# Second feed-forward's up part as seven block products, and 384-token groups throughout

## The chip, the core and the metric

The kernel runs on one core of a Trainium2 chip. The metric is the device time of one execution in microseconds (us). The core has TensorE (matmuls, PE; its weight loads are shown apart as PEld), VectorE (DVE), ScalarE (ACT), GpSimd (POOL) and SyncE (SP), which issues the transfers. Each engine runs its own queue in order; an instruction that needs another engine's result waits at the head of its queue, and everything behind it waits too.

## What is computed

Three parts follow each other on 1536 tokens (two sequences of 768) of width 320.

```python
x = mlstm(q, k, v, i_gate, f_gate, o_gate)          # gated linear attention, 8 heads of 40
x = x.transpose(0, 2, 1, 3).reshape(1536, 320)
# first feed-forward, d_ff = 1536
xn = x / sqrt(mean(x * x) + 1e-6) * rms_g
g, val = xn @ w_gate, xn @ w_val
x = (g * sigmoid(g) * val) @ w_out
# second feed-forward, d_ff = 2048
h = x @ w_in                                         # "up": 320 -> 2048
out = maximum(0.01 * h, h) @ w_out2                  # "down": 2048 -> 320
```

All is float32. The kernel keeps float32 accuracy with TensorE's faster `float32r` type by splitting each operand into a rounded part (`h`, "high") and the remainder (`l`, "low") and adding three products: high x high, high x low, low x high.

## The kernel before

**Tokens and hidden units.** The 1536 tokens are 12 tiles of 128. The first feed-forward treats hidden blocks 0 to 7 in four groups of three tiles (384 tokens, `GA`), and hidden blocks 8 to 11 in three groups of four tiles (512 tokens, `GB`). The second feed-forward uses `GB` too: 3 groups of 512 tokens, 16 hidden blocks of 128.

**The up part of the second feed-forward** (`h_up`, line 568 through `up`): for each group and hidden block one chain of eight matmuls of 512 columns into one PSUM bank. Input width 320 is two blocks of 128, which take three matmuls each (rows 0 to 255 of the weight), and a rest of 64, whose high and low parts share one 128-row tile (`w[:, 4]`, two matmuls). ACT then applies the leaky maximum (`h_relu`, line 684), ACT rounds the result (`sh`, line 607) and DVE subtracts to get the remainder (`sl`, line 613). The first feed-forward's up part (tiles `g` and `v`) has the same eight-matmul chain in the same function.

**The down part** (`out_down`, lines 697 to 699): per hidden block and 128-token tile three matmuls of 320 columns. Eight hidden blocks are added up in PSUM (`oa`), then kept in SBUF: the first half by an ACT copy, the second half by a DVE addition (`out_keep`, lines 707 and 709). That is 12 copies and 12 additions in all. Then `out_store` sends each tile out.

**PSUM** has eight banks, used as four pairs by tags `gv`, `o`, `acc`, `s`.

**Weights** arrive as 64-bit floats and are turned into float32 by three steps (`to_f32`: a DVE shift, an ACT rescale, a DVE merge), then split by an ACT cast and a DVE subtraction. `weight_a` makes the up weights (`wA`), `weight_b` the down weights (`wB`), `weight_r` the rest tiles.

**The order of the work** is the text `ORDER`: a list of tokens such as `H.0.3` (up of group 0, block 3), `R`, `S`, `L` (leaky maximum, rounding, remainder), `O` (down), `OK` (keep), `dO` (store). `play` calls them one by one, and each engine executes its share in just that order.

Of the kernel before, what the change touches and what calls it, by code (L numbers as in the profile page):

```python
# [7 lines left out]
F32 = mybir.dt.float32  # L8
# [33 lines left out]
GB = ((0, 4), (4, 8), (8, 12))  # L42
# [35 lines left out]
T.1.5 av.10.0 av.10.1 E.1.5 inn.10 abs.10 rec.10 th.10 y1.10 yr.10 U.1.5.1 M.1.5 arg.11.0 S.1.5 S.1.7 U.2.2.0 L.1.5
T.2.2 L.1.7 U.2.1.0 T.2.1 E.2.1 sq.10 p.11.1 E.2.2 de.11 xn.9 D.1.1.0 K.1.1.0 U.2.1.1 M.2.1 U.2.2.1 S.2.1 M.2.2
U.2.0.0 L.2.1 T.2.0 E.2.0 D.1.1.2 K.1.1.2 wA.9 U.2.0.1 M.2.0 D.1.1.1 y2.10.0 S.2.2 y2.10.1 K.0.1.1 K.1.1.1 b.9 th.11  # L80
eq.11 S.2.0 L.2.0 U.2.3.0 T.2.3 L.2.2 U.2.3.1 xc.9 tp.9 xh.9 p.11.0 av.11.0 av.11.1 wR.5 E.2.3 M.2.3 S.2.3 y2.10.2
inn.11 L.2.3 D.2.0.1 abs.11 rec.11 y1.11 yr.11 sq.11 K.2.0.1 D.2.0.0 xn.10 D.2.0.2 y2.11.0 xc.10 xl.9 y2.11.1 y2.11.2
xn.11 xc.11 tp.10 tp.11 close U.2.4.0 a.10 a.10 wA.8 a.8 b.9 a.8 wR.4 xh.10 U.2.5.0 xl.10 wA.12 T.2.4 E.2.4 U.2.4.1
M.2.4 xh.11 xl.11 S.2.4 L.2.4 b.9 a.8 a.8 T.2.5 E.2.5 U.2.7.0 r.4 U.2.5.1 U.3.2.1 a.12 r.4 r.4 U.3.2.0 T.2.7 M.2.5
a.12 K.2.0.0 E.2.7 r.4 U.2.7.1 M.2.7 U.2.6.0 a.12 S.2.5 L.2.5 a.9 a.9 S.2.7 U.2.6.1 T.2.6 E.2.6 M.2.6 U.3.0.1 S.2.6
a.12 wA.14 K.2.0.2 U.3.0.0 L.2.6 L.2.7 D.2.1.2 a.9 T.3.2 E.3.2 wA.17 M.3.2 U.3.3.0 D.2.1.0 T.3.0 a.14 a.14 a.9 K.2.1.2
a.14 wB.8 a.14 E.3.0 M.3.0 r.5 wA.11 S.3.0 L.3.0 wR.6 a.17 T.3.3 D.2.1.1 E.3.3 U.3.3.1 r.5 S.3.2 M.3.3 a.17 S.3.3
# [36 lines left out]
def body(ctx: ExitStack, tc, ig, fg, qk, nat, wgv, wgr, wo1, wi2, wi2r, wo2, rg, cst, cst2, out):  # L124
# [407 lines left out]
    def weight_b(key):
# [9 lines left out]
        else:  # L542
            w = slot("wB", [128, 2 * DM], key - NF, f"wB_{key}")
# [282 lines left out]
```

## Time and profile before

| | |
|---|---|
| median of three runs | 461.98 us (460.37 to 462.34) |
| the profiled execution | 458.02 us, of which 456.2 us from its first to its last instruction |
| mean granted TensorE clock | 0.977 |
| PE busy | 441.6 us (97%), 3566 instructions |
| DVE busy | 270.4 us (59%), 593 instructions |
| ACT busy | 232.3 us (51%), 549 instructions |
| POOL busy | 53.1 us (12%), 86 instructions |

Busy time of PE is not the measure of a matmul's cost here: the trace gives each 512-column matmul a duration of 395 ns, but they overlap, and what counts is the distance from one start to the next. The second feed-forward's up matmuls run from 267 us to about 440 us, mixed with the down matmuls.

### The profile page before, as it was taken

To read this page: it belongs to the slowest core of one execution; us is meant where nothing else is said; L and a number is where in the kernel's file an instruction comes from. 1 tells how busy PE (TensorE), PEld (TensorE's weight loads), DVE (VectorE), ACT (ScalarE), POOL (GpSimd) and SP (SyncE) were. 2 spreads that over 40 slices of the span, in tenths; PEclk is the share of its full clock that TensorE was granted. 3 is DMA by queue.
4 is the path that set the end of the run, shared out by engine and by line. 5 is a ranking of instruction groups with operands and counts; after the bars stand their busy time and mean duration, and the time that the engine had idled before them with its cause. 6 is when DMAs were issued, how large, how long until landed. Compare 5 with 4: busy or idle time off the path is not lost.

```text
span 456.2 us, 8986 instructions
## 1 busy us (share of the span) xinstructions
PE 441.6 (97%) x3566; PEld 393.6 (86%) x3568; DVE 270.4 (59%) x593; ACT 232.3 (51%) x549; POOL 53.1 (12%) x86
## 2 busy tenths in 40 slices
PE   9977979999999999999999999999999999999996
PEld 5764879999999999998887888988988888989896
DVE  5698998688776678785767785434603222221331
ACT  4686857666752365474435445544634444153150
POOL 4434552431110100000000000000000000000000
PEclk8579999999999999999999999999999999999999
DMA  7899894855810014331142110010101000010201
GB/s 284 298 303 269 274 317 121 252 191 140 215 70 1 2 55 171 109 99 57 35 146 98 31 57 30 29 30 0 59 0 31 29 2 0 1 43 1 72 1 58
DMA packets 21034, 45.43 MB, mean 100 GB/s; under 512 B 2128, under 2 KB 9168, under 8 KB 20992
## 3 DMA queue, kind: packets, MB, share of 16 engines
q1 hardware_dynamic: 20992, 44.85, 31.3%
q8 instruction: 28, 0.46, 0.4%
q14 instruction: 14, 0.11, 0.1%
HBM read 42.79 MB, written 2.06 MB: 98 GB/s over the span
## 4 chain that ended last, share of the span: by engine, by line
PE 91%; DVE 4%; ACT 2%; issue 1%; ACTq 0%; DVEq 0%
PE h L568 20%; PE g L568 15%; PE v L568 14%; PE xa L631 10%; PE oa L699 6%; PE oa L697 6%; PE oa L698 6%; PE xw L649 5%; PE s L290 2%; PE o L350 1%; PE A L216 1%; PE busy L181 1%; PE o L360 1%; DVE w L337 1%; ACT w L306 1%
## 5 line engine op out<-in xcount | busy, mean ns | idle before, releaser
L568 PE MATMUL h<-X,wA 128*128 128x512 f32 x384 | 93.2, 395 | 0.0
L568 PEld LDWEIGHTS h<-X,wA 128*128 128x128 f32 x384 | 71.4, 188 | 15.7
L613 DVE TENSOR_TENSOR sl<-u,sh 128x512 fp32r<-128x512 f32 x48 | 32.8, 691 | 87.0 <-ACT sh L607 87.0
L568 PE MATMUL v<-X,wA 128*128 128x384 f32 (+1 forms) x352 | 73.7, 355 | 1.5 <-ACT X L458 0.7
L568 PE MATMUL g<-X,wA 128*128 128x384 f32 (+1 forms) x352 | 74.1, 355 | 0.0
L568 PEld LDWEIGHTS v<-X,wA 128*128 128x128 f32 x352 | 62.5, 188 | 6.6 <-DVE th L601 1.0
L568 PEld LDWEIGHTS g<-X,wA 128*128 128x128 f32 x352 | 62.2, 188 | 5.2 <-DVE th L597 0.6
L684 ACT ACTIVATE u<-h 128x512 f32<-128x512 f32 x48 | 28.6, 598 | 67.5 <-PE h L568 55.3
L698 PE MATMUL oa<-wB,sh 128*128 128x320 f32 x192 | 59.3, 309 | 0.0
L699 PE MATMUL oa<-wB,sl 128*128 128x320 f32 x192 | 59.3, 309 | 0.0
L697 PE MATMUL oa<-wB,sh 128*128 128x320 f32 x192 | 59.3, 309 | 0.0
L631 PE MATMUL xa<-sh,wB 128*128 128x384 f32 x160 | 45.6, 337 | 0.0
L607 ACT CAST sh<-th 128x384 fp32r<-128x384 f32 (+1 forms) x44 | 23.5, 542 | 36.4 <-DVE th L601 30.3
L698 PEld LDWEIGHTS oa<-wB,sh 128*128 128x128 f32 x192 | 36.0, 188 | 0.9
L697 PEld LDWEIGHTS oa<-wB,sh 128*128 128x128 f32 x192 | 36.0, 188 | 0.9
L607 ACT CAST sh<-u 128x512 fp32r<-128x512 f32 x48 | 29.6, 620 | 13.6 <-PE oa L698 12.6
L699 PEld LDWEIGHTS oa<-wB,sl 128*128 128x128 f32 x192 | 36.0, 188 | 0.0
L590 ACT ACTIVATE th<-g 128x384 f32<-128x384 f32 (+1 forms) x44 | 22.9, 520 | 25.3 <-PE g L568 20.9
L601 DVE SCALAR_TENSOR_TENSOR th<-th,v 128x384 f32<-128x384 f32 (+1 forms) x44 | 25.8, 589 | 12.6 <-PE v L568 11.4
L631 PE MATMUL xa<-sl,wB 128*128 128x384 f32 x96 | 32.3, 336 | 0.0
L597 DVE SCALAR_TENSOR_TENSOR th<-th,g 128x384 f32<-128x384 f32 (+1 forms) x44 | 25.8, 586 | 9.7 <-ACT th L590 9.7
L631 PEld LDWEIGHTS xa<-sh,wB 128*128 128x128 f32 x160 | 29.3, 188 | 0.4
(111 smaller groups left out, 605.5 us busy)
## 6 DMA issues: line engine op xcount, KB each, us to landing
raw_B<-wo SPq DMA_DIRECT2D x28, 320.0 KB, 3.0
qkt<-qk SPq DMA_DIRECT2D x12, 512.0 KB, 6.7
raw_A<-wgv SPq DMA_DIRECT2D x12, 512.0 KB, 5.6
nat<-nat SPq DMA_DIRECT2D x12, 484.0 KB, 6.9
Ab<-A_d SPq DMA_DIRECT2D x10, 512.0 KB, 6.4
raw_A<-wi SPq DMA_DIRECT2D x8, 512.0 KB, 3.7
eb<-e_d SPq DMA_DIRECT2D x20, 128.0 KB, 8.0
out<-x SPq DMA_DIRECT2D x12, 160.0 KB, 1.9
```

The costliest lines, as they stand in the source:

```text
L568: PE.matmul(dst, a, x, start=(i == 0), stop=(i == len(seq) - 1))
L590: A.activation(th, u[0], AF.Tanh, scale=0.5)
L597: V.scalar_tensor_tensor(out=u["t"], in0=u["t"], scalar=1.0, in1=u[0], op0=ALU.add, op1=ALU.mult)
L601: V.scalar_tensor_tensor(out=u["t"], in0=u["t"], scalar=0.5, in1=u[1], op0=ALU.mult, op1=ALU.mult)
L607: A.copy(u["h"], u["t"])
L613: V.tensor_tensor(u["l"], u["t"], u["h"].bitcast(F32), op=ALU.subtract)
L631: PE.matmul(xa, w, x, start=(k == 0), stop=(k == len(seq) - 1))
L649: PE.matmul(xas["w", g, i], a, x, start=(f == NE and k == 0), stop=(f == NF - 1 and k == len(seq) - 1),)
L684: A.activation(t, u[0], AF.Prelu, alpha=0.01)
L697: PE.matmul(dst, sh[:, ts], wb[:, 0:DM], start=first, stop=False)
L698: PE.matmul(dst, sh[:, ts], wb[:, DM:], start=False, stop=False)
L699: PE.matmul(dst, sl[:, ts], wb[:, 0:DM], start=False, stop=last)
```

## The change

The up part of the second feed-forward now treats two groups of 384 tokens (a pair) and two blocks of 128 hidden units together. With weights `a11, a12` (to the first hidden block) and `a21, a22` (to the second), the second digit being the input block, and inputs `b11, b21` (first group) and `b12, b22` (second group), the 2 x 2 x 2 block product of the 256 main inputs takes seven products of blocks instead of eight (Strassen's scheme in Winograd's form). A product still is three matmuls. It needs sums of weight blocks (`s1` to `s4`, made by GpSimd), sums of input blocks (`t1` to `t4`, made by DVE) and running sums of products: bank `u[0]` accumulates one product after another, and is copied out by ACT three times in between (`c11`, `c21`, `c22`), and DVE adds the other banks to these copies (`h_sum`). The 64 rest inputs keep their two matmuls per hidden block and group.

Around that: `GB` is now `GA` (384 tokens everywhere, four groups); the outer loop of the second feed-forward is over 8 pairs of hidden blocks for all tokens, so a down chain adds up two hidden blocks in PSUM and is then kept, 8 times per tile (12 ACT copies and 84 DVE additions); the up weights of the second feed-forward are made one pair of hidden blocks after the other and reuse 8 + 4 slots; more buffers (`TB`, `SBL` = 8); and `ORDER` is another list from its 572nd token on (`M.0.7` before). Of it one line is shown.

```diff
-GB = ((0, 4), (4, 8), (8, 12))
+GB = GA
+PAIRS = ((0, 1), (2, 3))
+NK = DFF2 // 256
+SBL = 8
+TB = 8
...
-X.2.0 X.2.1 H.2.4 R.1.5 S.1.17 L.1.17 O.1.5 b.22 b.23 R.2.4 S.2.16 H.2.1 R.2.1 S.2.13 L.2.13 O.1.6 H.2.2 O.1.7
+R.1.0.3 H.0.1.1 OK.0.0.3 R.1.0.1 S2.1.0.1 X.1.1 L2.1.0.1 S2.1.0.3 R.1.0.2 O.0.0.1 H.0.1.0 HS.0.1.0 L2.1.0.3 X.1.6
...
+    def weight_s(key):
+        x = yield from to_f32(raws["A", key], 512, f"A{key}")
+        ...
+        G.tensor_tensor(q[0], a21, a22, op=ALU.add)
+        G.tensor_tensor(q[1], q[0], a11, op=ALU.subtract)
+        G.tensor_tensor(q[2], a11, a21, op=ALU.subtract)
+        G.tensor_tensor(q[3], a12, q[1], op=ALU.subtract)
+        A.copy(a[:, 0:128], a11)
+        A.copy(a[:, 128:384], x[:, 1])
+        V.tensor_tensor(a[:, 384:512], a11, a[:, 0:128].bitcast(F32), op=ALU.subtract)
+        V.tensor_tensor(a[:, 512:768], x[:, 1], a[:, 128:384].bitcast(F32), op=ALU.subtract)
+        ...
+        A.copy(a[:, 768:896], q[0])
+        A.copy(b[:, 0:384], sc[:, 128:512])
+        V.tensor_tensor(a[:, 896:1024], q[0], a[:, 768:896].bitcast(F32), op=ALU.subtract)
+        V.tensor_tensor(b[:, 384:768], sc[:, 128:512], b[:, 0:384].bitcast(F32), op=ALU.subtract)
...
+    def product(dst, k, p, a, b, first, last):
+        (ah, al), (bh, bl) = LEFT[NF + k][a], RIGHT[p][b]
+        for j, (x, y) in enumerate(((ah, bh), (ah, bl), (al, bh))):
+            PE.matmul(dst, x, y, start=first and j == 0, stop=last and j == 2, skip_group_check=not first)
+    def rest(dst, k, p, m, e, again):
+        PE.matmul(dst, w, X[:, 2, cs], start=False, stop=False, skip_group_check=again)
+        PE.matmul(dst, w, X[:, 5, cs], start=False, stop=True, skip_group_check=again)
...
-    def h_up(g, f):
-        cs, w = span(GB[g])
-        us[g, NF + f] = {0: psum(f"h{g}_{f}", "gv" if f % 2 else "o")[:, 0:w]}
-        up(us[g, NF + f][0], WA[NF + f // 2], f % 2, cs)
+    def h_up(k, p, i):
+        if i == 0:
+            product(h_bank(k, p, 0), k, p, "a11", "b11", True, True)
+        elif i == 1:
+            product(h_bank(k, p, 1), k, p, "s3", "t3", True, True)
+        elif i == 2:
+            product(h_bank(k, p, 2), k, p, "a12", "b21", True, False)
+            rest(u[2], k, p, 0, 0, False)
+        elif i == 3:
+            product(u[0], k, p, "s2", "t2", False, True)
+        elif i == 4:
+            product(h_bank(k, p, 3), k, p, "a22", "t4", True, False)
+            rest(u[3], k, p, 1, 0, False)
+        elif i == 5:
+            product(u[0], k, p, "s1", "t1", False, True)
+        elif i == 6:
+            rest(u[1], k, p, 1, 1, True)
+        else:
+            product(u[0], k, p, "s4", "b22", False, False)
+            rest(u[0], k, p, 0, 1, True)
+    def h_sum(k, p, i):
+        if i == 0: A.copy(u["c11"], u[0])
+        elif i == 1: V.tensor_tensor(u["c11"], u[2], u["c11"], op=ALU.add)
+        elif i == 2: A.copy(u["c21"], u[0])
+        elif i == 3: V.tensor_tensor(u["c21"], u[1], u["c21"], op=ALU.add)
+        elif i == 4: V.tensor_tensor(u["c21"], u[3], u["c21"], op=ALU.add)
+        elif i == 5: A.copy(u["c22"], u[0])
+        else: V.tensor_tensor(u["c22"], u[1], u["c22"], op=ALU.add)
...
+    def out_down(k, p, i):
+        for m in range(2):
+            PE.matmul(oa, v["h"][:, ts], wb[:, 0:DM], start=m == 0, stop=False)
+            PE.matmul(oa, v["h"][:, ts], wb[:, DM:], start=False, stop=False)
+            PE.matmul(oa, v["l"][:, ts], wb[:, 0:DM], start=False, stop=m == 1)
+    def out_keep(k, p, i):
+        if k == 0: A.copy(dst, oas[k, p, i])
+        else: V.tensor_tensor(dst, oas[k, p, i], dst, op=ALU.add)
```

TensorE before, about halfway through the second feed-forward: `h` is an up bank, `oa` a down bank, `wA` and `wB` the weights; the brackets name the engine whose result a row waits for.

```order
L568 MATMUL h_0_4280<-X,wA_2733 128x512 [waits Activation_49]
L568 MATMUL h_0_4280<-X,wA_2733 128x512 x7
L568 MATMUL h_5_4297<-X,wA_2832 128x512 x8
L568 MATMUL h_13_4308<-X,wA_3460 128x512 [waits Activation_49]
L568 MATMUL h_13_4308<-X,wA_3460 128x512 x7
L697 MATMUL oa_0_0_4323<-wB_3300,sh_12_4291 128x320 [waits Activation_49]
L698 MATMUL oa_0_0_4323<-wB_3300,sh_12_4291 128x320
L699 MATMUL oa_0_0_4323<-wB_3300,sl_12_4293 128x320 [waits DVE_49]
L697 MATMUL oa_0_1_4327<-wB_3300,sh_12_4291 128x320
L698 MATMUL oa_0_1_4327<-wB_3300,sh_12_4291 128x320
L699 MATMUL oa_0_1_4327<-wB_3300,sl_12_4293 128x320
```

Three whole chains of eight stand behind each other, each into a bank of its own, and a chain waits only for its bank to come free, before its first matmul.

TensorE now, the start of hidden pair 5 (the behind `h` stand the token pair, the bank and a serial number; `wS` and `T` hold the sums of weights and of inputs):

```order
L780 MATMUL h_0_2_5046<-X,wA_4704 128x384 x3
L785 MATMUL h_0_2_5046<-X,wA_4704 128x384
L786 MATMUL h_0_2_5046<-X,wA_4704 128x384
L780 MATMUL h_0_1_5055<-T_4_3680,wS_4986 128x384 [waits Activation_49]
L780 MATMUL h_0_1_5055<-T_5_3711,wS_4986 128x384
L780 MATMUL h_0_1_5055<-T_4_3680,wS_4986 128x384 [waits DVE_49]
L780 MATMUL h_0_0_5030<-T_4_3680,wS_4986 128x384 x3
L780 MATMUL h_0_3_5063<-T_5_3711,wA_4704 128x384 x3
L785 MATMUL h_0_3_5063<-X,wA_4704 128x384
L786 MATMUL h_0_3_5063<-X,wA_4704 128x384
L780 MATMUL h_0_0_5030<-X,wA_4704 128x384 [waits Activation_49]
L780 MATMUL h_0_0_5030<-X,wA_4704 128x384 x2
```

A chain is now cut into pieces: bank 0 takes three matmuls, then five into bank 3, and then three into bank 0 again, which wait for ACT's copy of what it held.

ACT now, the same place (`c` the copies and running sums, `u` and `c` also the leaky maximum's results, `xh` the rounded ones, `raw` and `w` the weights):

```order
L842 ACTIVATE c_4_1_4968<-c_4_1_4968 128x384 [waits DVE_49]
L615 CAST wB_5024<-w_B_4918 128x320
L820 COPY c_5_0_5034<-h_0_0_5030 128x384 [waits PE_49]
L842 ACTIVATE u_1_1_5044<-h_1_0_4876 128x384 [waits PE_49]
L847 CAST xh_1_1_5052<-u_1_1_5044 128x384 [waits Activation_49]
L825 COPY c_5_0_5069<-h_0_0_5030 128x384 [waits PE_49]
L531 ACTIVATE raw_R_4812<-raw_R_4812 128x256 [waits DMAHW0_49]
L832 COPY c_5_0_5081<-h_0_0_5030 128x384 [waits PE_49]
L597 CAST wA_5097<-w_R_5073 64x256 [waits DVE_49]
L597 CAST wA_5098<-w_R_5073 64x256
L842 ACTIVATE c_5_0_5034<-c_5_0_5034 128x384
```

The three copies of line 820, 825 and 832, on which TensorE's next product depends, stand in one queue with the leaky maximum of the unit before and with weight conversions.

ACT before, in its second feed-forward:

```order
L684 ACTIVATE u_6_4030<-h_6_4015 128x512 [waits DVE_49,PE_49]
L607 CAST sh_18_4032<-u_6_4030 128x512 [waits Activation_49]
L684 ACTIVATE u_0_4045<-h_0_4036 128x512 [waits DVE_49,PE_49]
L607 CAST sh_12_4047<-u_0_4045 128x512 [waits Activation_49]
L493 ACTIVATE raw_B_3960<-raw_B_3960 128x320 [waits DMAHW3_49]
L684 ACTIVATE u_3_4102<-h_3_4055 128x512 [waits DVE_49,PE_49]
L544 CAST wB_4104<-w_B_4049 128x320 [waits DVE_49]
L493 ACTIVATE raw_B_4013<-raw_B_4013 128x320 [waits DMAHW4_49]
L607 CAST sh_15_4110<-u_3_4102 128x512 [waits Activation_49]
```

There ACT takes a finished bank once (line 684) and rounds it (line 607); TensorE comes back to that bank only for another block.

## Rows read from the trace of the kernel before

**Rows 1.** The page's part 4: the chain that ended last, by engine.

```profile
PE 91%; DVE 4%; ACT 2%; issue 1%; ACTq 0%; DVEq 0%
```

**Rows 2.** Windows: busy us (count) by engine, granted TensorE clock, DMA share, GB/s.

```profile
20.00:40.00 20.00, 14.82 (x314) 10.92 (x319) 18.79 (x53) 13.90 (x45) 7.78 (x13) 0.77 0.96 292
40.00:60.00 20.00, 18.76 (x423) 16.54 (x412) 17.32 (x49) 17.45 (x54) 11.11 (x16) 1.00 0.90 270
60.00:80.00 20.00, 17.36 (x308) 15.77 (x308) 18.44 (x45) 12.51 (x39) 7.48 (x12) 1.00 0.69 211
100.00:120.00 20.00, 20.00 (x241) 19.32 (x240) 16.34 (x47) 11.40 (x34) 2.52 (x5) 1.00 0.61 157
340.00:360.00 20.00, 20.00 (x106) 17.47 (x105) 5.14 (x10) 7.93 (x16) 0.00 (x0) 1.00 0.11 34
```

**Rows 3.** TensorE's waits from 69 to 452 us: waiter, releaser, total us, times, longest.

```profile
PE v L568 <- DVE th L601: 0.7, 1, 0.7
```

**Rows 4.** Chain of waits in time order: start us, us, what (count).

```profile
100.47 2.79 PE v L568 x16
...
173.95 0.57 DVE th L601
...
174.56 1.67 PE v L568 x8
...
248.41 2.11 PE g L568 x8
...
276.49 5.60 PE h L568 x24
...
307.33 5.47 PE xw L649 x24
```

**Rows 5.** Timeline of TensorE, 296 to 312 us: start us, us, line, instruction.

```profile
295.74 0.31 PE L699 MATMUL oa<-wB,sl 128*128 128x320 f32 x1
...
301.46 0.31 PE L699 MATMUL oa<-wB,sl 128*128 128x320 f32 x1
```

**Rows 6.** Groups by line and form: count, busy us, mean ns, idle before.

```profile
L495 DVE SCALAR_TENSOR_TENSOR w_B<-raw_B,w_B 128x320 uint32<-128x320 uint32 x28 | 14.1, 502 | 4.3 <-ACT raw_B L493 2.9 <-ACT u L684 0.5
...
L613 DVE TENSOR_TENSOR sl<-th,sh 128x384 fp32r<-128x384 f32 x32 | 17.4, 553 | 3.5 <-ACT sh L607 3.4
...
L607 ACT CAST sh<-th 128x384 fp32r<-128x384 f32 x32 | 16.0, 512 | 21.7 <-DVE th L601 17.7 <-PE xa L631 2.8 <-PE xw L649 1.0
...
L329 POOL TENSOR_TENSOR Kt<-nat,aeu 128x160 f32<-128x160 f32 x20 | 9.3, 486 | 14.1 <-DMA nat<-nat 5.5 <-PE o L372 4.8 <-DVE aeu L207 3.9
...
L546 DVE TENSOR_TENSOR wB<-w_B,wB 128x320 fp32r<-128x320 f32 x16 | 7.7, 489 | 5.5 <-ACT wB L544 5.5
...
L639 DVE TENSOR_TENSOR x<-xa,x 128x384 f32<-128x384 f32 x12 | 6.6, 552 | 2.5 <-PE xa L631 2.5
...
L637 ACT COPY x<-xa 128x384 f32<-128x384 f32 x12 | 5.7, 476 | 3.6 <-PE xa L631 3.6
...
L709 DVE TENSOR_TENSOR x<-oa,x 128x320 f32<-128x320 f32 x12 | 5.5, 490 | 17.1 <-PE oa L699 17.1
```

**Rows 7.** Timeline of VectorE, 22 to 40 us.

```profile
24.22 1.76 DVE L495 SCALAR_TENSOR_TENSOR w_A<-raw_A,w_A 128x512 uint32<-128x512 uint32 x1
...
31.25 0.69 DVE L495 SCALAR_TENSOR_TENSOR w_A<-raw_A,w_A 128x512 uint32<-128x512 uint32 x1
31.86 0.69 DVE L518 TENSOR_TENSOR wA<-w_A,wA 128x512 fp32r<-128x512 f32 x1
```

**Rows 8.** Timeline of GpSimd, 18 to 45 us.

```profile
24.16 1.27 POOL L314 TENSOR_TENSOR eb<-eb,qkt 128x512 f32<-128x512 f32 x1 [3.18 <-DMA eb<-e_d]
```

**Rows 9.** Timeline of all engines, 436 to 457 us.

```profile
437.59 0.19 PEld L697 LDWEIGHTS oa<-wB,sh 128*128 128x128 f32 x1
437.82 0.31 PE L697 MATMUL oa<-wB,sh 128*128 128x320 f32 x1
...
438.02 0.60 ACT L684 ACTIVATE u<-h 128x512 f32<-128x512 f32 x1 [1.22 <-PE h L568]
```

More of the change, by code (lines that the diff above doesn't have):

```diff
@@ L78 @@
[L78 to L87, printed above, removed]
@@ L542, in weight_b @@
         else:
-            w = slot("wB", [128, 2 * DM], key - NF, f"wB_{key}")
+            w = wpool.tile([128, 2 * DM], F32R, tag="wB", name=f"wB_{key}")
             A.copy(w[:, 0:DM], x)
@@ L605, in u_s @@
         n = u["t"].shape[1]
-        u["h"] = pools["ffn"].tile([128, ffn_n()], F32R, tag="sh", name=f"sh{g}_{f}", bufs=SB)[:, 0:n]
+        u["h"] = pools["ffn"].tile([128, 384], F32R, tag="sh", name=f"sh{g}_{f}", bufs=sb())[:, 0:n]
         A.copy(u["h"], u["t"])
@@ L686, in body @@
-    oas = {}
-    def out_down(g, f):
-        wb, h = WB[NF + f], f // (NF2 // 2)
-        sh, sl = us[g, NF + f]["h"], us[g, NF + f]["l"]
-        first, last = f % (NF2 // 2) == 0, f % (NF2 // 2) == NF2 // 2 - 1
-        for i in range(GB[g][1] - GB[g][0]):
-            if first:
-                oas[g, h, i] = psum(f"oa{g}_{h}_{i}", "acc" if i < 2 else "s")
-            ts = slice(i * L, (i + 1) * L)
-            dst = oas[g, h, i][:, 0:DM]
-            PE.matmul(dst, sh[:, ts], wb[:, 0:DM], start=first, stop=False)
-            PE.matmul(dst, sh[:, ts], wb[:, DM:], start=False, stop=False)
-            PE.matmul(dst, sl[:, ts], wb[:, 0:DM], start=False, stop=last)
@@ new lines, in h_sum @@
+    def h_sum(k, p, i):
+        u = us["H", k, p]
+        tile = lambda n: pools["ffn"].tile([128, 384], F32, tag="th", name=f"{n}_{k}_{p}")
+        if i == 0:
+            u["c11"] = tile("c11")
+            A.copy(u["c11"], u[0])
+        elif i == 1:
+            V.tensor_tensor(u["c11"], u[2], u["c11"], op=ALU.add)
+        elif i == 2:
+            u["c21"] = tile("c21")
+            A.copy(u["c21"], u[0])
+        elif i == 3:
+            V.tensor_tensor(u["c21"], u[1], u["c21"], op=ALU.add)
+        elif i == 4:
+            V.tensor_tensor(u["c21"], u[3], u["c21"], op=ALU.add)
+        elif i == 5:
+            u["c22"] = tile("c22")
+            A.copy(u["c22"], u[0])
+        else:
+            V.tensor_tensor(u["c22"], u[1], u["c22"], op=ALU.add)
@@ new lines, in h_relu, with h_s, h_l @@
+    def h_relu(k, p, o):
+        u = us["H", k, p]
+        us["h", k, p, o] = v = {}
+        src = u[0] if o == 1 else u[("c11", "", "c21", "c22")[o]]
+        v["t"] = t = src if o != 1 else pools["ffn"].tile([128, 384], F32, tag="th", name=f"u{k}_{p}_{o}")
+        A.activation(t, src, AF.Prelu, alpha=0.01)
+    def h_s(k, p, o):
+        v = us["h", k, p, o]
+        v["h"] = pools["ffn"].tile([128, 384], F32R, tag="sh", name=f"xh{k}_{p}_{o}", bufs=SBL)
+        A.copy(v["h"], v["t"])
+    def h_l(k, p, o):
+        v = us["h", k, p, o]
+        v["l"] = pools["ffn"].tile([128, 384], F32R, tag="sl", name=f"xl{k}_{p}_{o}", bufs=SBL)
+        V.tensor_tensor(v["l"], v["t"], v["h"].bitcast(F32), op=ALU.subtract)
@@ L713, in out_store, with part @@
+    def part(p, i):
+        return x2[:, tile_of(p, i)].rearrange("p k l -> p (k l)")[:, 0:DM]
+    def out_keep(k, p, i):
+        dst = part(p, i)
+        if k == 0:
+            A.copy(dst, oas[k, p, i])
+        else:
+            V.tensor_tensor(dst, oas[k, p, i], dst, op=ALU.add)
+    def out_store(p, i):
+        c, b = divmod(tile_of(p, i), B)
         r0 = b * S + c * L
-        Q.dma_start(out=out[r0:r0 + L, :], in_=part(g, i))
+        Q.dma_start(out=out[r0:r0 + L, :], in_=part(p, i))
```

215 lines of the change are left out of this document (151 added, 64 removed).

## The prediction

> **What bounds the kernel now.** I read the chain of waits first: 91% of it is TensorE [rows 1]. Then the windows of 20 us. From 100 us on TensorE is busy in every microsecond at a granted clock of 1.00, while VectorE goes from 16.34 of 20 us down to 5.14 in the second feed-forward; before 80 us it is the other way round, VectorE is nearly full and TensorE idles [rows 2]. The list of TensorE's waits shows a single one behind 69 us, 0.7 us long [rows 3]. So the second feed-forward is worth what its matmuls cost from start to start, and any wait that the change puts on TensorE is paid in full.
>
> The prices from start to start: 16 matmuls of 384 columns in 2.79 us, 0.1744 us each; 24 `h` matmuls of 512 columns in 5.60 us, 0.2333 each; 24 `xw` matmuls of 512 in 5.47 us, 0.228 each [rows 4]; 39 matmuls of 320 columns from 295.74 to 301.46 us, 0.1467 each [rows 5]. That is 0.454 ns a column at 384, 0.456 at 512, 0.458 at 320: no fixed part per matmul to be seen, so narrower groups are not dearer by themselves.
>
> **The change part by part.** *Up part.* Before: 3 groups x 16 blocks x 8 = 384 matmuls of 512 columns, 384 x 0.2333 = 89.6 us. Now, for each of 8 hidden pairs and 2 token pairs, 7 products x 3 + 4 rests x 2 = 29 matmuls of 384 columns (the same columns took 32 before): 464 x 0.1744 = 80.9 us. Saved: 8.7 us. *Narrower groups.* The last four hidden blocks of the first feed-forward: 192 x 0.2333 = 44.8 us become 256 x 0.1744 = 44.6 us; their `xw` sums 96 x 0.228 = 21.9 us become 128 x 0.1744 = 22.3 us. Together +0.2 us. The down part keeps its 576 matmuls of 320 columns. *Sum on TensorE: 8.5 us less.*
>
> Here the rows and the Trainium skill differ: "TensorE: Matmul & The Clock Gate", section "Back-to-back issue gap", gives N/2.4 + 2.5 ns between starts, so a fixed part per matmul. By it 384 columns take 162.5 ns and 512 take 215.8, and the up part would save 82.9 - 75.4 = 7.5 us, the narrower groups cost 0.3 us, in all 7.2 us. The trace shows 174.4 and 233.3 ns, proportional to the columns, and I take the trace.
>
> *The one old wait.* At 173.95 us TensorE stood behind VectorE's `th` (0.57 us and its handovers), and the eight matmuls behind it took 1.67 us where eight take 1.40 [rows 4]: 0.9 us. In the new order no `U` follows that closely behind the `M` that frees its bank; only the block `D.2.0.1` follows `L.2.3` with nothing to spare. I take 0.9 us off and put 0.3 us on. Up to token 571, about 118 us, nothing has moved.
>
> *New waits on TensorE.* Bank 0 is used four times in a row in each of the 16 units, and TensorE must wait for ACT's copy each time. The bare turnaround: ACT started 0.20 us behind the end of the last start-to-start step (437.82 to 438.02), and a weight load stands 0.23 us ahead of its matmul (437.59 to 437.82) [rows 9]; the copy takes 0.476 us [rows 6]; with 0.04 us back to TensorE (174.52 to 174.56, behind VectorE) [rows 4] this is 0.72 us, and 0.95 us if the weight load waits with its matmul. Between the two uses TensorE has other work. Of the 55 places where the order names such a wait on ACT, 15 have five matmuls of 384 or six of 320 in between (0.87 to 0.88 us), 11 have 1.2 to 1.4 us, 29 have 1.75 us or more. So 15 places are tight. Lower bound nothing (the weight load doesn't wait); upper bound 0.08 us each, and half of an ACT instruction of 0.512 us [rows 6] in front: 0.34 us x 15 = 5.1 us. The nearest rows are two places of before with a similarly close release: eight matmuls that took 2.11 us where eight of 512 take 1.87, 0.24 us lost [rows 4], and the wait above. At most of these places the instruction ahead of the copy in ACT's queue has its inputs a product or more earlier, so I stay below those and take 0.14 us each: 2.1 us.
>
> *VectorE.* Line 852 (remainder) 64 x 0.553 = 35.4 us, the adds of `h_sum` 64 x 0.552 = 35.3 us, the keeps 84 x 0.490 = 41.2 us, and 104 others, mostly weights, at the 0.489 us of a weight's subtraction, 50.9 us [rows 6]: 163 us behind the first `h` matmul. Back to back an instruction of 0.69 us starts 0.61 us behind the last [rows 7], so 144 us if they never wait. TensorE needs there 464 x 0.1744 + 32 x 0.1744 (the last `xw`) + 576 x 0.1467 = 171 us. So VectorE goes from a quarter (5.14 of 20) to 84 to 95%. ACT, 48 copies x 0.476 + 128 x 0.512 + some 84 others at the same 0.512, has 131 us, 77%. In the windows of before, 82% of VectorE (16.34 of 20) left TensorE full, 87% (17.32) came with 1.24 us idle in 20 [rows 2]. The closest place where TensorE waits for VectorE has 1.4 us in between against a bare 1.03 us (0.20 + 0.552 + 0.04 + 0.23), the next ones 1.75 us; a queue of one or two instructions eats that. Bounds: 0, and the pace of the 87% window for all of the stage, 171 x 20/18.76 - 171 = 11.3 us. I stay near the 82% row and take 1.5 us.
>
> *GpSimd* adds 24 subtractions and additions of 128 columns in the stage, below 0.486 us each [rows 6], on no chain of TensorE while the weights are a unit or more ahead. But one VectorE instruction that began while GpSimd worked from 24.16 to 25.43 us took 1.76 us, the same one without GpSimd 0.69 [rows 7, 8]. The Trainium skill, "SBUF — State Buffer", section "Who interferes with whom", says that a VectorE instruction with two SBUF inputs contends with a GpSimd instruction that reads SBUF; this trace agrees, 1.76 against 0.69 us. So up to 24 x 0.486 = 11.7 us of VectorE time could go: covered while VectorE has its 27 us to spare (171 - 144), and a cause of the third rival if not.
>
> *Covered.* The four sums of `t` per pair and the splits run while other products fill TensorE; the weights' transfers ride on queues that moved 34 GB/s in this stage [rows 2]. The end is as before: last down matmul, one keep, one store. Nothing is booked for them; without cover a pair's sums would cost 4 x 0.553 = 2.2 us once each.
>
> *Sum:* -8.5 - 0.9 + 0.3 + 2.1 + 1.5 = -5.5 us. Profiled execution 458.02 us, so 452.5 us. That execution lies 0.9% below the median shown, 461.98 us; against the median: **456.5 us**.
>
> **Rivals.** *All waits hidden.* For it: no place has less than 0.87 us in between, more than the 0.72 us. Against it: 0.95 us with the weight load. Then -8.5 - 0.9 + 0.3 = -9.1: 452.9 us.
>
> *The turnarounds eat it.* ACT is at 77%, and in the order shown the copies stand behind weight rescales and the leaky maximum. If the 15 tight places lose 0.34 us, the 11 next ones 0.2 us and VectorE's queue costs 1.5 us: 5.1 + 2.2 + 1.5 = 8.8 us, result -0.3: 461.7 us, no change.
>
> *VectorE becomes the bound of the second feed-forward.* Its price is the pace of the 87% window, +11.3 us, in place of my waits: -9.1 + 11.3 = +2.2: 464.2 us, slower; at the pace of the row from 60 us (17.36 of 20) it is +26.0 and 478.9 us. It decides from where VectorE's waits for ACT and TensorE and GpSimd's port exceed its 27 us to spare. For it: before 80 us just this is seen. Against it: there the attention's own chain ran through VectorE, here it feeds work that TensorE needs a unit later.
>
> *No saving in the matmuls:* that there are 464 instead of 512 of 384 columns stands in the code; only a dearer start could undo it, and the equal prices per column speak against it: 3%, shared out to "no change".
>
> **How the numbers follow.** 0.54 for the forecast, with its own range 454.0 to 459.3 (waits of 1.1 to 6.4 us); 0.15 all hidden; 0.19 eaten (with the 3%); 0.12 VectorE bound. The range reaches from the all-hidden case, 452.8, past the eaten one to 462.6 us, and leaves out the VectorE case and a little below. About 0.5% is what a measurement of this kernel tells from no change: below 459.7 us is faster, above 464.3 slower. Faster: 0.15 + 0.54 x 0.95 + 0.04 of the eaten case = 0.70. Slower: 0.10 of the VectorE case, whose price begins at that bound. No change: the rest, 0.20.
>
> **What would show it.** `h` starts 0.174 us apart within a product; waits on TensorE only on lines 820, 825, 832 and 842 of ACT, each below 0.3 us and 2 to 3 us in all; VectorE at 84 to 90% of the second feed-forward, its idle time in front of `h_sum` put down to PE or ACT; no wait at 174 us. It would be wrong if TensorE's waits name VectorE's lines 822 to 852 or 878 with more than 4 us, if the granted clock falls below 1.00 in that stage, or if `h` starts stand further apart than 0.18 us.

## The result, and the profile after

The changed kernel takes 450.21 us (median of 4 runs, 449.32 to 450.78), the kernel before in the same comparison 461.32 us (460.37 to 462.34). The ratio is 0.9757, 95% interval 0.9726 to 0.9788: faster by 2.1 to 2.7%. Forecast were 456.5 us and a range of 452.8 to 462.6, so the sign was right, the gain twice as large as predicted, and the time 2.6 us below the range. The profiled execution took 449.84 us, 448.1 us of it from the first to the last instruction.

The page's part 1 (busy time, share of the span, instructions) and part 4 (compare [rows 1]):

```profile
PE 436.2 (97%) x3742; PEld 418.5 (93%) x3744; DVE 346.8 (77%) x802; ACT 262.4 (59%) x672; POOL 70.9 (16%) x118
...
PE 93%; DVE 3%; ACT 2%; issue 2%; ACTq 0%; DVEq 0%
```

The windows that answer to [rows 2], in the same columns, and the whole stretch from the first `h` matmul to the last matmul:

```profile
20.00:40.00 20.00, 15.97 (x282) 11.95 (x285) 17.76 (x49) 12.94 (x42) 7.35 (x11) 0.62 0.92 278
...
100.00:120.00 20.00, 20.00 (x242) 19.32 (x241) 16.76 (x48) 12.34 (x37) 5.85 (x10) 1.00 0.51 175
340.00:360.00 20.00, 20.00 (x128) 19.97 (x127) 17.66 (x43) 13.11 (x32) 1.89 (x4) 1.00 0.18 64
...
273.00:444.40 171.40, 171.40 (x1074) 171.05 (x1073) 140.52 (x313) 112.81 (x262) 12.45 (x24) 1.00 0.13 42
```

The forecast's 171 us of TensorE work came out as 171.4 us. VectorE rose from 5.14 to 17.66 of 20 us, but over the stage it is at 140.5 of 171.4 us (82%) and ACT at 112.8 (66%); neither makes TensorE wait. The list of TensorE's waits from 60 us to the end, which answers to [rows 3], has three entries, all before 81 us, and none in the second feed-forward:

```profile
PE tp L492 <- DVE X L500: 2.5, 1, 2.5
PE g L639 <- DVE th L665: 0.6, 1, 0.6
PE tp L492 <- ACT xn L485: 0.2, 1, 0.2
```

**A fixed stretch to compare.** Up to token 571 the two kernels run the same instructions, yet the start varies: the 129th `s` matmul began at 77.64 us before and at 79.68 us after. So I measure from that matmul to the start of the last one. The timeline of before, then of after:

```profile
77.64 1.16 PE L290 MATMUL s<-qkt 40*128 40x128 f32 x16
...
451.86 0.31 PE L699 MATMUL oa<-wB,sl 128*128 128x320 f32 x1
```

```profile
79.68 1.16 PE L328 MATMUL s<-qkt 40*128 40x128 f32 x16
...
444.41 0.31 PE L868 MATMUL oa<-wB,xl 128*128 128x320 f32 x1
```

Before 374.22 us, after 364.73: **9.49 us less**. Adding up the start-to-start steps by tile, `h` gives 8.18 of it (89.50 to 81.32), `g` and `v` 1.40 (119.03 to 117.63; the wait at 174 us of [rows 4] is gone), `xw` and `xa` cost 0.28, the down part is the same (84.33 and 84.31). These distances also settle what the list of waits alone can't, since it shows only 0.57 of a bare turnaround's 0.85 us (below): the 464 `h` steps take 81.32 us where 464 x 0.1744 are 80.92, and the down part takes what it took before, so all waits of TensorE in the second feed-forward together come to some 0.4 us. From the last matmul's start to the end of the span it is 4.39 us before and 3.66 after, another 0.73. Against that the start took 2.04 us more in this execution.

### The profile page after: what moved, and what is told of

Read it like the earlier page. It is cut to its first block, busy times and chain, and to the rows that moved or that the text cites. A ratio compares the mean times of both kernels' runs of the same rounds, so it can differ in the third digit from the quotient of the medians.

```text
span 448.1 us, 9631 instructions
## 1 busy us (share of the span) xinstructions
PE 436.2 (97%) x3742; PEld 418.5 (93%) x3744; DVE 346.8 (77%) x802; ACT 262.4 (59%) x672; POOL 70.9 (16%) x118
## 4 chain that ended last, share of the span: by engine, by line
PE 93%; DVE 3%; ACT 2%; issue 2%; ACTq 0%; DVEq 0%
PE g L639 14%; PE v L639 14%; PE h L780 13%; PE xa L702 10%; PE oa L866 6%; PE oa L867 6%; PE oa L868 6%; PE xw L720 5%; PE s L328 3%; PE h L786 3%; PE h L785 2%; PE o L388 2%; PE busy L219 2%; PE A L254 1%; PE o L398 1%
## 5 line engine op out<-in xcount | busy, mean ns | idle before, releaser
L639 PE MATMUL g<-X,wA 128*128 128x384 f32 x384 | 74.2, 339 | 0.6 <-DVE th L665 0.6
L639 PE MATMUL v<-X,wA 128*128 128x384 f32 x384 | 74.3, 338 | 0.4 <-ACT X L496 0.2
L866 PE MATMUL oa<-wB,xh 128*128 128x320 f32 x192 | 59.4, 309 | 0.0
L867 PE MATMUL oa<-wB,xh 128*128 128x320 f32 x192 | 59.3, 309 | 0.0
L868 PE MATMUL oa<-wB,xl 128*128 128x320 f32 x192 | 59.2, 308 | 0.0
L878 DVE TENSOR_TENSOR x<-oa,x 128x320 f32<-128x320 f32 x84 | 39.4, 485 | 11.7 <-PE oa L868 11.5
L669 DVE SCALAR_TENSOR_TENSOR th<-th,v 128x384 f32<-128x384 f32 x48 | 26.3, 551 | 15.7 <-PE v L639 15.1
L665 DVE SCALAR_TENSOR_TENSOR th<-th,g 128x384 f32<-128x384 f32 x48 | 26.2, 549 | 13.2 <-ACT th L661 13.0
L866 PEld LDWEIGHTS oa<-wB,xh 128*128 128x128 f32 x192 | 36.0, 188 | 0.1
L868 PEld LDWEIGHTS oa<-wB,xl 128*128 128x128 f32 x192 | 36.0, 188 | 0.0
L867 PEld LDWEIGHTS oa<-wB,xh 128*128 128x128 f32 x192 | 36.0, 188 | 0.0
L780 PE MATMUL h<-X,wA 128*128 128x384 f32 x144 | 32.8, 337 | 0.0
```

Source lines behind the costliest of these rows:

```text
L639: PE.matmul(dst, a, x, start=(i == 0), stop=(i == len(seq) - 1))
L665: V.scalar_tensor_tensor(out=u["t"], in0=u["t"], scalar=1.0, in1=u[0], op0=ALU.add, op1=ALU.mult)
L669: V.scalar_tensor_tensor(out=u["t"], in0=u["t"], scalar=0.5, in1=u[1], op0=ALU.mult, op1=ALU.mult)
L780: PE.matmul(dst, x, y, start=first and j == 0, stop=last and j == 2, skip_group_check=not first)
L866: PE.matmul(oa, v["h"][:, ts], wb[:, 0:DM], start=m == 0, stop=False)
L867: PE.matmul(oa, v["h"][:, ts], wb[:, DM:], start=False, stop=False)
```

## The experiments

All are made from the changed kernel, but for the last. "Stretch" is the one above; the difference is to the changed kernel's 364.73 us. The ratios are to the kernel before, run beside each.

| run | stretch us | difference | median us | ratio to before (95%) |
|---|---|---|---|---|
| eight plain products | 374.28 | +9.55 | 459.42 | 1.0013 (0.9978 to 1.0049) |
| turnaround uncovered, 16 times | 378.80 | +14.07 | 464.11 | 1.0094 (1.0056 to 1.0132) |
| all 48 copies doubled | 372.91 | +8.18 | 458.03 | 1.0024 (0.9978 to 1.0069) |
| 14 tight copies doubled | 370.83 | +6.10 | 454.55 | 0.9877 (0.9806 to 0.9949) |
| the other 34 doubled | 366.63 | +1.90 | 451.27 | 0.9828 (0.9776 to 0.9880) |
| 32 roundings doubled (ACT) | 368.23 | +3.50 | 452.55 | 0.9853 (0.9770 to 0.9935) |
| 64 roundings doubled (ACT) | 375.30 | +10.57 | 460.07 | 1.0010 (0.9973 to 1.0046) |
| 32 remainders doubled (VectorE) | 369.74 | +5.01 | 454.36 | 0.9899 (0.9848 to 0.9949) |
| the same 32, read by nobody | 366.97 | +2.24 | 452.03 | 0.9822 (0.9759 to 0.9885) |
| 64 remainders doubled (VectorE) | 380.61 | +15.88 | 466.21 | 1.0169 (1.0116 to 1.0223) |
| the kernel before, again | 374.07 | | 461.55 | one run |

**Without the seven products.** `h_up` makes four chains of eight again, at the places where the seven-product scheme finishes its banks.

```diff
-        if i == 0:
-            product(h_bank(k, p, 0), k, p, "a11", "b11", True, True)
...
+        if i in (2, 4, 6, 7):
+            j, m, e = {2: (2, 0, 0), 4: (3, 1, 0), 6: (1, 1, 1), 7: (0, 0, 1)}[i]
+            up(h_bank(k, p, j), WA[NF + k], m, span(GB[PAIRS[p][e]])[0])
```

> All of the change except the seven products: the same order, groups of 384, hidden pairs and keeps, but the up part is again eight block products, plain chains of eight matmuls (512 instead of 464 matmuls of 384 columns), without the sums of weights and inputs, ACT's copies and the additions of products. Theory A (the gain is TensorE's shorter up part and nothing else of size): 48 x 0.1744 = 8.4 us slower than the changed kernel's 450.2 us, so about 458.6 us, within 1 us of before less its old waits and tail. Rival B (the other order of the work gave the gain by removing waits): no more than 3 us slower than the changed kernel. Rival C (the seven products also cost hidden waits of some 3.6 us, as predicted): only 4.8 us slower, 455 us.

The stretch is 374.28 us, that of before 374.22, and the ratio of the times is 1.00: the other order, the groups of 384 and the hidden pairs by themselves give nothing on balance. This run has the 1.40 us at `g` and `v` too (117.63), but against before it loses 0.49 at `h` (89.99) and 0.90 in the down part (85.23). The seven products turn that into the whole gain, 9.55 us: 48 matmuls x 0.1744 = 8.4, and some 1.2 us of waits that this run has and the changed kernel hasn't, 0.3 at `h` and 0.9 in the down part by the same steps. TensorE's waits from 200 us on show 0.8 of it:

```profile
PE oa L838 <- DVE x L850: 0.5, 1, 0.5
PE oa L840 <- DVE xl L824: 0.3, 1, 0.3
```

Theory A holds, and rival C, hidden waits of 3.6 us in the changed kernel, is out.

**The turnaround of bank 0, bare.**

```diff
-H.0.0.3 HS.0.0.2 H.0.0.4 FX.3.1 R.0.0.0 FX.3.2 H.0.0.5
+H.0.0.3 HS.0.0.2 H.0.0.5 H.0.0.4 FX.3.1 R.0.0.0 FX.3.2
```

and likewise in the other 15 units, in most of them with ACT's copy (`HS`) moved up as well, so that it stands between the two products. In one unit (hidden pair 0, second token pair) the moved product now reads the place of its rounded input sum before that is written.

> The same matmuls, but in each of the 16 units the product s1 x t1 into bank 0 is put straight behind the product s2 x t2 into bank 0, so that nothing covers ACT's copy between the two: TensorE's wait for the copy lies bare 16 times. Theory A (the turnaround is what the trace of the changed kernel shows at a tight place: 0.20 us to ACT, 0.48 us copy, 0.05 us back, 0.13 us of weight load, 0.86 us in all, and ACT's queue is free): 16 x 0.86 = 13.8 us slower than the changed kernel, 464.0 us. Rival B (the prediction's: weight load 0.23 us ahead, and half an ACT instruction in front of the copy): 16 x (0.95 + 0.26) = 19.4 us slower, 469.6 us. Rival C (the weight load doesn't wait, 0.72 us): 11.5 us slower, 461.7 us.

14.07 us, 0.88 a place, and 0.85 by the steps of `h` alone (13.62 us in 16 places): theory A (0.86), not the prediction's 1.21 or 0.72. TensorE's wait list from 269 us on shows all 16 places in one row, the only one; behind it one of the places in the timeline of all engines:

```profile
PE h L672 <- ACT c L717: 9.1, 16, 0.6
```

```profile
381.26 1.21 PE L672 MATMUL h<-T,wS 128*128 128x384 f32 x6
...
382.51 0.48 ACT L717 COPY c<-h 128x384 f32<-128x384 f32 x1 [0.88 <-PE h L672]
...
383.04 0.47 PEld L672 LDWEIGHTS h<-X,wA 128*128 128x128 f32 x3 [0.89 <-ACT c L717]
383.04 0.80 PE L672 MATMUL h<-X,wA 128*128 128x384 f32 x3 [0.57 <-ACT c L717]
...
383.50 0.54 PEld L672 LDWEIGHTS h<-T,wA 128*128 128x128 f32 x3
383.68 0.51 PE L672 MATMUL h<-T,wA 128*128 128x384 f32 x2
```

Six steps of 0.1744 from 381.26 end at 382.31; ACT starts 0.20 us later, TensorE at 383.04, 0.73 us after the step's end. The three matmuls then take 0.64 us where three take 0.52: the weight load that had no lead costs 0.12. Together 0.85. The list shows only 0.57 of it, since the modelled end of a matmul lies behind its step.

**Which copies are tight.** ACT copies bank 0 twice in a row, at all 48 places, then at the 14 which my count had as covered with 0.87 or 0.88 us of matmuls, then at the other 34.

```diff
             A.copy(u["c21"], u[0])
+            if (k, p, i) in TIGHT:
+                A.copy(u["c21"], u[0])
```

> ACT copies bank 0 twice in a row at each of the 48 places (the second copy writes the same values over the first), so that each turnaround of bank 0 grows by one copy of 0.48 us, from 0.86 to 1.34 us; ACT has 23 us more. By the order of the matmuls, 14 of the 48 turnarounds are covered by 0.87 or 0.88 us of other matmuls, 7 by 1.22 to 1.40, 27 by 1.75 us or more. Theory A (a tight place of the changed kernel is covered to within 0.02 us and ACT's queue in front of the copies is short): 14 x 0.48 + 3 x 0.12 = 7.1 us slower than the changed kernel from the same early matmul to the last one. Rival B (copies queue behind other ACT work, so that the places between 1.2 and 1.8 us are hit too): 10 us or more. Rival C (the turnaround is hidden at the tight places by more than the matmuls between): 2 us or less.

> ACT copies bank 0 twice at the 14 places whose turnaround is covered by just 0.87 or 0.88 us of other matmuls, and once at the other 34. Theory A (these places are covered to within 0.02 us, so each added copy is paid): 14 x 0.48 = 6.7 us slower than the changed kernel from the same early matmul to the last. Rival B (the 8.2 us that all 48 doubled copies cost came from a fuller ACT queue everywhere): 14/48 of them, 2.4 us.

> ACT copies bank 0 twice at the 34 places with 1.22 us or more of other matmuls to cover the turnaround, and once at the 14 with 0.87 or 0.88 us. Theory A (what lies beyond 1.34 us is free, three places of 1.22 lose 0.12 us): 0.4 us slower than the changed kernel, up to 1.5 us with what the 34 copies delay in ACT's queue. Rival B (a fuller ACT queue everywhere): 34/48 of 8.2 us, 5.8 us.

The 14 places cost 6.10 us, the 34 others 1.90; together 8.00 against 8.18 for all 48, which lies between theory A (7.1) and rival B (10 or more), nearer to A. TensorE's waits, in the run with the 14 and in that with the 34:

```profile
PE h L781 <- ACT c L830: 1.0, 5, 0.2
PE h L781 <- ACT c L823: 0.8, 4, 0.2
PE h L781 <- ACT c L839: 0.8, 4, 0.2
```

```profile
PE h L781 <- ACT c L839: 0.2, 1, 0.2
PE h L781 <- ACT c L823: 0.2, 1, 0.2
```

Theory A holds, and the tight places are 13, not 14. At the first copy of the first unit, which the run's list has as tight, 32 `xw` matmuls stand in between as well (5.55 us, in a row further down); it is the one place of the 14 without a wait. At the 13 the matmul behind the copy comes 0.46 to 0.48 us later, for a copy of 0.48, so the cover of the unchanged kernel exceeds its turnaround by 0.02 us at most; against the bare 0.85 us it would be 0.02 to 0.03. The 34 cost a little more than the 0.4 to 1.5 us expected, and 1.6 of their 1.90 us fall on four places.

**More work in ACT's queue.** The cast of line 847 twice, for every second tile or for every tile.

```diff
         A.copy(v["h"], v["t"])
+        if o % 2:
+            A.copy(v["h"], v["t"])
```

> The rounding of the leaky maximum's result is done twice for every tile, 64 more ACT instructions of 0.51 us, 32.8 us; the values stay. ACT's share of the stage behind the first h matmul goes from 113 of 171 us (66%) to 146 (85%). Theory A (the copies of bank 0 stand in a short queue, and what TensorE waits for is mostly further than 1.7 us away): 1 to 4 us slower than the changed kernel, by an extra instruction in front of some of the 14 tight copies. Rival B (the prediction's: a copy already waits for half an instruction in front of it, and twice as often now): 14 x 0.26 = 3.6 us more for the copies, and the remainders and down matmuls late as well, 8 us or more in all. Rival C (no place is tight for ACT): no change, less than 1 us.

> The rounding of the leaky maximum's result is done twice for every second tile, 32 more ACT instructions of 0.51 us, 16.4 us; ACT's share of the stage goes from 66 to 76%. With all 64 doubled it was 10.6 us slower. Theory A (each added instruction is paid when a copy stands behind it, so the cost goes with their number): 5.3 us. Rival B (ACT's queue costs little until it is filled to some 80%): 2 us or less.

10.57 us with 64 casts more, which is rival B's total there, and 3.50 with 32, between the two theories. TensorE's waits behind 81 us, with 64:

```profile
PE h L780 <- ACT c L820: 3.8, 5, 1.4
PE h L780 <- ACT c L832: 0.6, 2, 0.4
PE h L780 <- ACT u L842: 0.5, 1, 0.5
```

Lines 820 and 832 are copies of bank 0. So instructions in front of a copy do hold TensorE, as the prediction argued, and for up to 1.4 us. Rival B's premise, that a copy already waits for half an instruction in the changed kernel, isn't borne out: its `h` steps leave 0.4 us for all waits. By the distances between starts some 9 of the 10.6 us lie in front of `h` matmuls and under 2 in front of down matmuls.

**More work in VectorE's queue.**

```diff
         V.tensor_tensor(v["l"], v["t"], v["h"].bitcast(F32), op=ALU.subtract)
+        if o % 2:
+            V.tensor_tensor(v["l"], v["t"], v["h"].bitcast(F32), op=ALU.subtract)
```

for 32, without the condition for 64, and for the third run with a tile of its own, which nobody reads, as output.

> The remainder's subtraction is done twice for every second tile, 32 more VectorE instructions of 0.55 us, 17.7 us; the value stays. VectorE's share of the stage behind the first h matmul goes from 140 of 171 us (82%) to 158 (92%). Theory A (VectorE costs nothing until its instructions no longer fit into TensorE's time): at most 1 us slower than the changed kernel's 450.2 us. Rival B (the prediction's: from some 87% on VectorE's queue holds TensorE at the pace of the window from 40 us): 10 us or more slower, 460 us or above.

> The remainder's subtraction is done twice for every tile, 64 more VectorE instructions of 0.55 us, 35.4 us; the value stays. VectorE then needs 140 + 35 = 176 us where TensorE needs 171. Theory A (VectorE becomes the bound just when it is full): 4.5 us slower than the changed kernel if its instructions pack without a gap, up to 12 us with gaps and the run-in, so 455 to 462 us, and TensorE's waits name VectorE. Rival B (waits begin well below a full VectorE): 20 us or more slower, 470 us and above. Rival C (VectorE's 140 us hold waits of its own inside the durations, which shrink under pressure): less than 2 us slower.

> The same 32 more VectorE instructions of 0.55 us as in the run with 32 doubled subtractions, at the same places in the queue, but written to a tile that nobody reads, so that no result is later by its own second instruction and only what stands behind it in the queue is. That run lost 5.0 us from the same early matmul to the last. Theory A (the loss is VectorE's queue: at 91% of the stage it holds TensorE): again 4 to 6 us. Rival B (the loss was the later remainder, on which TensorE's down matmuls wait directly): 2 us or less.

5.01, 15.88 and 2.24 us: the first two fall between the theories, the third is close to rival B. The stage in the three, in windows from the first `h` on: with 32 doubled, with the 32 that nobody reads, and with 64, this one with the largest rows of TensorE's waits behind it:

```profile
274.00:450.30 176.30, 174.01 (x1074) 170.74 (x1072) 155.71 (x345) 113.34 (x262) 12.30 (x24) 1.00 0.12 41
```

```profile
273.40:447.00 173.60, 172.65 (x1073) 170.70 (x1072) 153.01 (x345) 113.14 (x262) 12.30 (x24) 1.00 0.12 41
```

```profile
273.20:460.20 187.00, 178.06 (x1073) 170.50 (x1072) 172.94 (x377) 114.04 (x262) 12.07 (x24) 1.00 0.12 38
```

```profile
PE oa L869 <- DVE xl L853: 4.2, 8, 1.9
PE oa L867 <- DVE x L879: 1.8, 3, 0.9
PE h L785 <- DVE c L827: 1.4, 3, 0.6
```

At 88% (155.71 of 176.30, 153.01 of 173.60) VectorE costs 2 to 5 us, more than half of the larger figure because the remainder itself is late for the down matmuls; at 92% (172.94 of 187.00) it is busy for longer than TensorE's own 171 us and sets the pace, with 14 us still idle. The share alone is not the price: at one share the two runs with 32 differ by 2.8 us.

**The kernel before, again.** No edit.

> The kernel before, once more, for its start. In the profiled runs so far the instructions up to the 129th s matmul are the same, and it started 77.6 us (before), 79.7 (changed kernel), 78.0, 76.1, 80.5 and 79.5 us (four variants) behind the span's start. Theory A (the start varies from run to run by some 4 us, whatever the kernel, and the rest does not): anything from 76 to 81 us to that matmul, and 374.2 us within 0.3 from there to the last matmul, as in the profile of before. Rival B (before has a shorter start of its own): 77.6 us within 0.3.

Start at 81.37 us, 0.4 us above theory A's span, and stretch 374.07: theory A, not rival B. The stretch repeats to 0.15 us, and over all the profiled runs of this study the start lay between 73.6 and 81.4 us.

## Why the prediction was wrong

*Up part, narrower groups: right.* Of the 8.7 us forecast for the up part, the tile `h` shows 8.18, and making the eight products again costs 9.55, of which 8.4 are the 48 matmuls. The step stays what [rows 4] gave: 32 `xw` matmuls of 384 columns in 5.55 us, 0.1734 each, in the chain of after:

```profile
274.43 5.55 PE xw L720 x32
```

The Trainium skill's N/2.4 + 2.5 ns for N columns ("TensorE: Matmul & The Clock Gate", section "Back-to-back issue gap"), which that section ties to single matmuls and not to a stream with weight loads, would be 162.5 ns by estimate; the trace goes on disagreeing with it.

*Old wait: right in kind, somewhat more.* 0.9 off and 0.3 on were booked; `g` and `v` give back 1.40 us, and no wait came at the block that I had feared. Not one wait is listed behind 81 us.

*New waits on TensorE, 2.1 us: this step failed.* I priced the turnaround at 0.72 or 0.95 us, against covers of 0.87, and took 0.14 us a place. It is 0.86, and what it costs is next to nothing: 0.4 us for all waits of the stage. By the order 14 places are tight, 13 copies and one leaky maximum; the count behind my 15 took in the first unit's first copy. A tight place in the timeline of the changed kernel, all engines:

```profile
375.83 1.23 PE L780 MATMUL h<-T,wS 128*128 128x384 f32 x6
...
376.90 0.68 PE L780 MATMUL h<-T,wA 128*128 128x384 f32 x3
...
377.10 0.48 ACT L825 COPY c<-h 128x384 f32<-128x384 f32 x1 [0.90 <-PE h L780]
...
377.42 0.33 PE L785 MATMUL h<-X,wA 128*128 128x384 f32 x1
...
377.59 0.34 PE L786 MATMUL h<-X,wA 128*128 128x384 f32 x1
377.63 0.50 PEld L780 LDWEIGHTS h<-X,wA 128*128 128x128 f32 x3
377.76 0.69 PE L780 MATMUL h<-X,wA 128*128 128x384 f32 x3
```

The last three of the six go into bank 0, and their last step ends at 376.90; the copy starts 0.20 us later and ends at 377.58; the weight load goes at 377.63 and the matmul at 377.76, exactly five steps behind 376.90. The lead of the weight load has shrunk to 0.13 us without delaying anything; my 0.23 came from [rows 9], where it followed the 512-column matmuls of `h` and nothing pressed it. The second half of the price, an ACT instruction in front of the copy, was a real mechanism (the runs with more casts), but in the changed kernel, with ACT at 66%, it cost nothing that the steps show. I had 77% by summing durations to 131 us; the instructions overlap in the trace, and the engine is busy 112.8.

*VectorE, 1.5 us: failed too.* The share was near (82% against 84 to 95), the price is nothing that the steps show. I had read it off windows of the attention [rows 2], where the chain of waits runs through VectorE's and ACT's work before TensorE can go on, as in this chain of before (`X` is what TensorE reads):

```profile
43.05 0.70 DVE w_R L495
...
45.12 0.57 DVE X L462
45.73 1.50 PE v L568 x7
```

The bare 1.03 us for VectorE adds up to 1.02, and nothing hangs on it. For "the 87% window's pace" I had 11.3 us; at 88% the runs measured 2.2 and 5.0.

*The end: "as before" was wrong by 0.73 us.* The timeline of the last keeps and stores before, then after:

```profile
450.88 1.81 DVE L709 TENSOR_TENSOR x<-oa,x 128x320 f32<-128x320 f32 x4 [6.27 <-PE oa L699]
...
451.40 2.05 SPq L714 DMA_DIRECT2D out<-x  x4
```

```profile
442.63 2.97 SPq L883 DMA_DIRECT2D out<-x  x5
...
443.88 0.49 DVE L878 TENSOR_TENSOR x<-oa,x 128x320 f32<-128x320 f32 x1 [0.39 <-PE oa L868]
...
444.75 0.49 DVE L878 TENSOR_TENSOR x<-oa,x 128x320 f32<-128x320 f32 x1 [0.39 <-PE oa L868]
```

Before, the last four tiles are kept back to back and their stores leave in one go; after, they are spread over 3 us. That this is the cause wasn't tried, and the run with plain products, which has the later order of keeps, also took 4.29 us from its last matmul.

*The sum.* 456.5 missed 450.2 by 6.3 us. 3.6 of them are waits that weren't there, 0.73 the end, and 0.4 the stretch (9.49 against 9.1), in all 4.7. Of the other 1.6 us, 0.66 are the reference's own scatter, from 461.98 to 461.32 us, the median in the comparison. The last 0.9 is what is left over; different starts can give that much, but this isn't shown, since only the profiled runs show their start. "All waits hidden" is the rival that came true in its mechanism. I gave it 0.15, since 0.95 us stood against a cover of 0.87. Its 452.9 us, on which the range ended, was still 2.7 us too high: the end, the stretch and these 1.6 us again.

## What to carry to other kernels

Where TensorE is full at clock 1.00 and its queue has other work, matmuls taken away are gained one for one, and even a cover that beats a turnaround by two hundredths of a us holds: price the turnaround from its parts, and let the weight load's lead shrink. Price a fuller engine by which of its results TensorE waits for and how far ahead they are made, not by its share of another stage. Where the start of a program varies, compare from an instruction behind it.

## What the runs showed of the hardware

**The start.** The same instructions up to the 129th `s` matmul took 73.6 to 81.4 us. The granted clock there differs from run to run: windows of before, then of its second profile (columns as in [rows 2]).

```profile
20.00:30.00 10.00, 6.85 (x185) 5.21 (x185) 9.41 (x26) 7.71 (x26) 3.83 (x6) 0.84 0.96 287
...
40.00:50.00 10.00, 8.76 (x233) 7.33 (x225) 8.04 (x22) 8.67 (x27) 5.68 (x7) 1.00 0.89 241
```

```profile
20.00:30.00 10.00, 8.94 (x153) 6.43 (x153) 7.99 (x24) 6.52 (x22) 2.75 (x4) 0.50 0.89 287
...
40.00:50.00 10.00, 9.88 (x162) 8.18 (x158) 7.22 (x22) 7.65 (x24) 4.70 (x8) 0.66 0.72 213
```

At 0.50, the level of 1.2 GHz, TensorE was at work in 8.94 of 10 us and did fewer matmuls (153 against 185); the run with the low clock reaches the mark 3.73 us later. The clock isn't all of it: up to the mark its mean was 0.87 before (77.64 us) and 0.77 in the second profile (81.37 us), but 0.78 in the run with all 48 copies doubled, which began at 76.27 us. Why one run gets the higher clock earlier stays open.

**GpSimd beside VectorE.** A remainder of 0.55 us took 0.82 while GpSimd formed weight sums, whose own times went from 0.47 to 0.78 us (timeline of the changed kernel, both engines):

```profile
302.16 0.55 DVE L852 TENSOR_TENSOR xl<-c,xh 128x384 fp32r<-128x384 f32 x1
...
303.12 0.78 POOL L572 TENSOR_TENSOR sums<-sums,w_A 128x128 f32<-128x128 f32 x1
303.49 0.82 DVE L852 TENSOR_TENSOR xl<-c,xh 128x384 fp32r<-128x384 f32 x1
...
304.60 0.47 POOL L574 TENSOR_TENSOR sums<-w_A,sums 128x128 f32<-128x128 f32 x1
```

Additions of `h_sum`, which read one operand from PSUM, stayed at their 0.55 us. The Trainium skill ("SBUF — State Buffer", section "Who interferes with whom") says that a VectorE instruction with two SBUF inputs contends with a GpSimd instruction that reads SBUF, and that one with at most one SBUF input, outside the 2-port modes, doesn't; the trace agrees. Of the nine VectorE instructions with two SBUF inputs that ran beside GpSimd's in this stage, five took 0.23 to 0.30 us longer and four kept their time. In all it cost VectorE some 1.3 us here, far from the 11.7 us that I had set as the bound.
